# Routed attention and sorted experts on one core: a second GpSimd drain, another order of the first loads, and four smaller moves

## The chip, the cores and the metric

One core of a Trainium2 chip. Its engines are called here by the profile's names beside their own: PE (TensorE, matmuls), PEld (its weight loads), DVE (VectorE), ACT (ScalarE), POOL (GpSimd) and SP (SyncE, which here only issues transfers). The metric is the device time of one execution in microseconds. Times inside the trace are counted from the start of its span.

## The reference

Two blocks follow each other. The first is attention with a mask by clusters: each query and each key is assigned to the nearest of 16 centroids of its head, and a query only sees keys of the same cluster. The second is a layer of experts: a gate picks one of 8 experts for each of the 3072 tokens, and the token goes through that expert's two matrices.

```python
# q, k, v: (4 batches, 8 heads, 768, 64); centroids: (8, 16, 64); w1: (8, 512, 1024); w2: (8, 1024, 512)
q_assign = argmax(einsum("bhsd,hcd->bhsc", q_n, c_n), -1)   # q_n, k_n, c_n: rows divided by their norm
k_assign = argmax(einsum("bhsd,hcd->bhsc", k_n, c_n), -1)
mask = q_assign[:, :, :, None] == k_assign[:, :, None, :]
scores = where(mask, q @ k.T / 8, -1e9)
attn_out = softmax(scores) @ v
x = attn_out.transpose(0, 2, 1, 3).reshape(3072, 512)
expert_idx = argmax(x @ w_gate, 1); gate_w = softmax(x @ w_gate)[expert_idx]
y[t] = gate_w[t] * (relu(x[t] @ w1[expert_idx[t]]) @ w2[expert_idx[t]])
```

All of it is float32.

## The kernel before

**Attention.** The 16 pairs of heads (4 batches times 4 pairs) are worked off one after another. For pair n TensorE makes the scores of 12 blocks in fp32, adds the mask by a bf16 matmul of one-hot clusters (`mq`, `mk`, two buffers each, L370), ScalarE takes the exp (`A`, L383), VectorE adds the blocks up (`acc`, L389), and TensorE multiplies `A` with v (L395). Beside it, steps of the pairs to come are put between the blocks: the loads of pair n+2, the transposes of q and k (L262 for pair 0 on TensorE, L272 for the others on VectorE), the similarity to the centroids (`similar`, L304) and the one-hot clusters (`assign0` to `assign2`, `place`). In `place`, ScalarE copies the one-hot clusters of the queries into `mq` (L350, four copies a pair) and VectorE writes those of the keys into `mk` (L352).

A step is put in its place by `at_pair(n, u, f, ...)`: f is issued in pair n after block u (0 to 11 the score blocks, 12 and 13 in the attends). `sum_up` of the pair before (L415: the sums for the softmax and the gate's logits, in one PSUM bank), `weights_of` (VectorE reads that bank), `rows` and `store` (L452: the rows of x to HBM) go in this way, and so do the steps by which a batch's tokens are given to experts: `gate`, `gate_exp`, `gate_sum`, `choose` (whose last result is `last`, L521), `count` (two matmuls with 8 columns, L526 and L527, into a PSUM bank of its own out of the two of the pool `ps_m`), `number` (VectorE reads the counts, L532 and L533, and gets each token's place `pos_i`, L539; GpSimd then scatters the tokens into the list `tokens_of`, L541). `rank_first` and `first_turns` prepare the first turns from the first three batches.

**The start.** `load(0)` and `load(1)` are issued first: q and k of pair 0 in halves on SP's and ScalarE's queues (L183), v on SP's (L193), and then the eight transfers of pair 1 (L187) and its v. The centroids are normed and transposed (`cn`, `cT`), and stored in HBM as `cn_d` (L289). `routing_constants` lets GpSimd write constants (L138 to L160), among them `none`, with which SP fills `tokens_of` by eight transfers (L141).

**The experts.** The sorted tokens are worked off in ten turns: two of 288 columns from the first batches, and eight (256, 288, 288, 384, 416, 416, 448 and 128 columns), ordered by the experts' counts. A turn's layer 1 (L902) and layer 2 (L1003, L1022) are made by Strassen's scheme with seven products in place of eight, so VectorE makes sums of the weights (`w1_sums`, L723 with `a`; `w2_sums`, L723 with `v`), of the rows (`x_sums`) and of the hidden values (`h_sums`), and adds up the products (L860). The weights of a turn are fetched by `first_weights` (w1, 2 MB, L97) and `second_weights` (w2, 2 MB, L105), each in one of two buffers by the turn's parity. The tokens of a turn come by `places` (reads the list, `sf`, L646), `indices` (`gi`, `si`, L662), `gather` (GpSimd, `xg`, L672), `weigh` (L689, L695) and `take` (L705); `write` (L977) puts out the rows by GpSimd's indirect transfers. Here too a step has a place: `at(h1, i, ...)` in layer 1 of the turn, `at(h2, i, ...)` in layer 2. Buffers and semaphores follow from the order in which the steps are written; every engine executes its instructions in that order.

The last turn has 128 columns. It runs without Strassen; its output is one PSUM bank, which ScalarE copies to SBUF (L1029), GpSimd writes out, and after which every engine drains and the program ends (L1435).

Of the kernel before, what the change touches and what calls it, by code (L numbers as in the profile page):

```python
# [8 lines left out]
F32 = mybir.dt.float32  # L9
# [24 lines left out]
def kernel(  # L34
# [128 lines left out]
    with tc.manual_schedule(), ExitStack() as actx:  # L163
# [12 lines left out]
        def load(n):  # L176
            b, hp = divmod(n, HP)
            for d, src, name in ((QIN, q, "q_in"), (KIN, k, "k_in")):
                t = d[n] = ld.tile([P, NI, Q4], F32, name=name)
                if n == 0:  # L180
                    t = d[n] = t.rearrange("p i d -> p (i d)").rearrange("p (j a d) -> p j a d", a=2, d=D)
                    for a in range(2):
                        (nc.sync, nc.scalar)[a].dma_start(out=t[:, :, a, :], in_=src[0, a].rearrange("(p j) d -> p j d", j=NQ))  # L183
                    continue
                for r in range(4):
                    s = src[b, 2 * hp + r // 2, :, Q4 * (r % 2) : Q4 * (r % 2 + 1)]
                    nc.sync.dma_start(  # L187
                        out=t[Q4 * r : Q4 * (r + 1)].rearrange("t (j a) d -> t j a d", a=4),
                        in_=s.rearrange("(a t j) d -> t j a d", a=4, j=NQ),
                    )  # L190
            VIN[n] = ldv.tile([P, 2, NQ, D], F32, name="v_in")
            for a in range(2):
                nc.sync.dma_start(  # L193
                    out=VIN[n][:, a], in_=v[b, 2 * hp + a].rearrange("(p j) d -> p j d", j=NQ)
                )

        cin = consts.tile([P, D], F32)
        nc.scalar.dma_start(out=cin, in_=centroids.rearrange("h c d -> (h c) d"))
        for n in range(2):
            load(n)  # L200

# [9 lines left out]
        MK = [msk.tile([P, S], BF16, name=f"mk{i}") for i in range(2)]  # L211
        for i in range(2):
            for t in (MQ[i], MK[i]):
                (nc.gpsimd if i else nc.vector).memset(t, 0.0)

# [4 lines left out]
        for a in range(2):  # L220
# [3 lines left out]
            )  # L224
        make_identity(nc, ident)
        first_c = iota("first_c", [P, C], [[-1, C]], C, 0)
        ones_s = consts.tile([P, 2, Q4], F32)
# [57 lines left out]
        for a in range(2):  # L285
            nc.vector.tensor_copy(cT[D * a : D * (a + 1), :, a, :], cv[D * a : D * (a + 1), :, a, :])
        first_turn(1)
        for a in range(2):
            nc.scalar.dma_start(  # L289
                out=cn_d.rearrange("(h a) d c -> a d h c", a=2)[a], in_=cT[D * a : D * (a + 1), :, a, :]  # L290
            )
        first_cb = consts.tile([P, C], BF16)
        nc.vector.tensor_copy(first_cb, first_c)
        ksc2 = consts.tile([P, 2], F32)
        kscn2 = consts.tile([P, 2], F32)
        for r in range(4):
            nc.vector.tensor_copy(ksc2[Q4 * r : Q4 * (r + 1)], ksc)
            nc.vector.tensor_copy(kscn2[Q4 * r : Q4 * (r + 1)], kscn)

# [42 lines left out]
        def place(n, w):  # L342
            t, m = OH[n], (MQ, MK)[w][n % 2]
            for h in range(2):
                for a in range(2):
# [3 lines left out]
                    if w == 0:  # L349
                        nc.scalar.copy(dst, src)  # L350
                    else:
# [51 lines left out]


        def sum_up(n):

            ps = SL[n] = ps_m.tile([P, 512], F32, name="mps")
            for w in range(3):
                for qd in range(4):
# [112 lines left out]

        def count(b):
            last = LAST.pop(b)
            cps = CPS[b] = ps_m.tile([P, 512], F32, name="mps")
            nc.tensor.matmul(cps[:, 0:E], lhsT=lt_strict, rhs=last, start=True, stop=True)  # L526
# [234 lines left out]
        for n in range(NPAIR):  # L761
            if n:
                at_pair(n, 2, sum_up, n - 1)
                at_pair(n, 2, weights_of, n - 1)
                at_pair(n, 4, rows, n - 1)
# [3 lines left out]
        for b in range(B - 1):  # L769
# [3 lines left out]
            at_pair(n, 8 if last else 11, gate_exp, b)  # L773
            at_pair(n + (not last), 10 if last else 3, gate_sum, b)
            at_pair(n + (not last), 8 if last else 9, choose, b)
            at_pair(n + 2 - last, 0 if last else 4, count, b)
            at_pair(n + 2 - last, 1 if last else 6, number, b)
        n = HP * (B - 1)
        slots = range(len(EARLY))
        at_pair(n + 1, 3, rank_first)  # L780

# [46 lines left out]
    with tc.manual_schedule(), ExitStack() as ectx:  # L828
# [156 lines left out]
        def layer2(s, hooks):  # L985
# [28 lines left out]
            def tile_of(j):  # L1014
# [4 lines left out]
                for k in range(FB // n):  # L1019
# [6 lines left out]
                    if n == 1 and k % 2 and not pairs:  # L1026
                        hook()
                if n == 1:
                    nc.scalar.copy(z[0:m], ps[0:m])  # L1029
# [68 lines left out]
        for s in range(NS):  # L1098
# [5 lines left out]
            if s == 0:  # L1104
# [11 lines left out]
                at(h2, 0, rank_rest)  # L1116
                at(h2, 3, places, 2)
                at(h2, 7, indices, 2)
                at(h2, 7, gather, 2)
# [3 lines left out]
            if s < last:  # L1123
# [6 lines left out]
                if s == 1:  # L1130
                    at(h1, 6, weigh, 2)
                    at(h1, 7, take, 2)

                    at(h1, 7, first_weights, 2)
                    at(h1, 8, second_weights, 2)
# [7 lines left out]
                elif s == 1:  # L1143
                    when = ((h2, 2), (h2, 3), (h2, 4), (h2, 5), (h2, 6), (h2, 6))
                else:
# [17 lines left out]
            if pairs_of(s):  # L1163
                at(h1, 4, w2_sums, s, (1,), nc.vector)
                at(h1, 6, w2_sums, s, (3,), nc.vector)
            (layer1 if GR[s]["T"] >= 2 * P else few_columns)(s, h1)
            h_sums(s)
# [272 lines left out]
```

## Time and profile before

| | us |
|---|---|
| median of 3 runs | 679.32 |
| the runs | 682.28, 679.32, 677.63 |
| the profiled execution | 680.02 |
| its span | 678.2 |
| PE busy | 648.1 (96%) |
| DVE busy | 512.5 (76%) |
| ACT busy | 301.0 (44%) |
| POOL busy | 124.4 (18%) |
| mean granted clock of PE | 0.989 |

The first pair's scores begin at 11.9 us, a pair takes 19.7 us and some of those in which a batch is counted up to 22.2, the first turn's first matmul is at 339.3, and the last matmul ends at 666.5. A line of the profile names the source line, the engine, the operation with its output and inputs, how many times it ran, its busy time, and the idle time of its engine ahead of it with what ended that. The profiled execution is 1.8 us longer than its span; differences within the span are read from the trace and then set against the runs.

### The profile page before, as it was taken

Reading aid. Unit: us, or ns where it says so; the run is one execution under the profiler, and the core shown is the slowest. Engines: PE = TensorE matmul, PEld = TensorE weight load, DVE = VectorE, ACT = ScalarE, POOL = GpSimd, SP = SyncE. Lnnn points to the kernel's source line nnn. Section 1 sums busy time; section 2 is a strip of 40 time slices with the busy share of each in tenths; the row PEclk is TensorE's granted clock in tenths of the full one; section 3 lists DMA queues with packets and bytes.
Section 4 is the critical chain, followed back from the end, with each engine's and each line's share of the span. In section 5 each row is a group of like instructions: output and inputs, shape, how many; then the busy total and the mean of one; then the engine's idle time right before and its main releaser. Section 6 shows DMA issues by size and latency. Waiting matters only on the chain.

```text
span 678.2 us, 11364 instructions
## 1 busy us (share of the span) xinstructions
PE 648.1 (96%) x4210; PEld 424.3 (63%) x4210; DVE 512.5 (76%) x909; ACT 301.0 (44%) x524; POOL 124.4 (18%) x145
## 2 busy tenths in 40 slices
PE   4999999999999999999999989999999999999993
PEld 2445444455444454444484879978797977869771
DVE  5889999999999999999887788886868375562300
ACT  2756556667556566556432323333231332413210
POOL 4000000012000300222113522324241422040010
PEclk9899999999999999999999989999999999999997
DMA  9723455433455434356473498667494837523010
GB/s 185 144 51 73 88 94 94 67 70 69 80 94 94 73 73 78 63 152 197 113 264 96 147 388 281 227 261 251 196 288 175 271 127 218 201 73 135 7 49 17
DMA packets 191807, 95.37 MB, mean 141 GB/s; under 512 B 155967, under 2 KB 173887, under 8 KB 190464
## 3 DMA queue, kind: packets, MB, share of 16 engines
q1 hardware_dynamic: 184016, 81.12, 43.8%
q0 software_dynamic: 4928, 12.97, 5.8%
q10 hardware_dynamic: 2800, 0.48, 0.4%
q8 instruction: 35, 0.57, 0.4%
q14 instruction: 28, 0.23, 0.1%
HBM read 74.10 MB, written 20.70 MB: 140 GB/s over the span
## 4 chain that ended last, share of the span: by engine, by line
PE 52%; issue 27%; DVE 8%; DMA 5%; POOL 5%; SPq 2%; ACT 1%; POOLq 0%; DVEq 0%; ACTq 0%
PE sps L370 19%; PE mps L395 15%; PE bank L902 4%; PE bank L1003 3%; PE sbank L902 3%; POOL out_dram L977 3%; PE sbank L1003 2%; PE mps L415 2%; PE bank L1022 2%; PE mps L304 2%; DVE acc L389 2%; POOL xg L672 1%; DMA w<-in_moe_w_dram 1%; DVE a L723 1%; DVE xw L689 1%
## 5 line engine op out<-in xcount | busy, mean ns | idle before, releaser
L383 ACT ACTIVATE A<-sps 128x768 f32<-128x768 f32 x192 | 153.1, 811 | 47.3 <-PE sps L370 46.2
L370 PE MATMUL sps<-qT,kT 64*128 64x384 f32 x768 | 160.2, 496 | 1.9 <-ACT A L383 1.9
L389 DVE TENSOR_TENSOR acc<-acc,A 128x768 f32<-128x768 f32 x128 | 121.4, 948 | 9.7 <-ACT A L383 3.3
L395 PE MATMUL mps<-A,v_in 128*64 128x384 f32 x768 | 127.4, 488 | 0.0
L370 PEld LDWEIGHTS sps<-qT,kT 64*128 64x128 f32 x768 | 66.8, 188 | 57.8 <-issue 51.0
L395 PEld LDWEIGHTS mps<-A,v_in 128*64 128x64 f32 x768 | 53.8, 137 | 70.5 <-issue 62.2
L977 POOL DMA_INDIRECT out_dram<-z,si x30 | 47.8, 1594 | 199.9 <-DVE z L860 170.7
L541 POOL DMA_INDIRECT tokens_of<-tg,pos_i x24 | 27.1, 1128 | 291.8 <-DVE pos_i L539 145.8
L370 PE MATMUL sps<-mq,mk 64*128 64x384 bf16 x384 | 63.4, 324 | 2.7 <-ACT mq L350 2.7
L1022 PE MATMUL bank<-w,h 128*128 128x512 f32 (+2 forms) x224 | 64.4, 596 | 0.0
L672 POOL DMA_INDIRECT xg<-x_rows,gi x30 | 41.4, 1382 | 50.7 <-DVE gi L662 19.3
L350 ACT COPY mq<-ohT 32x384 bf16<-32x384 bf16 x64 | 32.6, 510 | 38.7 <-DVE ohT L340 29.5
L902 PE MATMUL sbank<-xc,a 128*128 128x144 f32 (+4 forms) x288 | 48.0, 310 | 1.4 <-ACT h L920 0.7
L902 PE MATMUL bank<-xT,w 128*128 128x144 f32 (+4 forms) x288 | 47.8, 309 | 0.0
L902 PEld LDWEIGHTS bank<-xT,w 128*128 128x128 f32 x288 | 43.9, 191 | 2.6 <-issue 2.2
L1022 PEld LDWEIGHTS bank<-w,h 128*128 128x128 f32 (+2 forms) x224 | 24.6, 151 | 32.5 <-issue 32.3
L902 PEld LDWEIGHTS sbank<-xc,a 128*128 128x128 f32 x288 | 43.3, 190 | 2.1 <-issue 1.2
L860 DVE TENSOR_TENSOR h<-sbank,p 128x288 f32<-128x288 f32 (+4 forms) x18 | 9.2, 513 | 46.8 <-PE sbank L902 45.7
L370 PEld LDWEIGHTS <-mk 64*128 64x128 bf16 x384 | 19.5, 94 | 28.2 <-DVE mk L352 3.3
L920 ACT ACTIVATE h<-h 128x288 f32<-128x288 f32 (+4 forms) x36 | 17.6, 488 | 41.4 <-DVE h L860 32.6
L689 DVE TENSOR_TENSOR xw<-xg,sf 128x256 f32<-128x256 f32 (+2 forms) x60 | 32.8, 607 | 2.2 <-DMA xg<-x_rows,gi 1.7
L389 DVE TENSOR_TENSOR acc<-A 128x768 f32<-128x768 f32 x32 | 30.3, 947 | 5.1 <-ACT A L383 5.0
(205 smaller groups left out, 884.5 us busy)
## 6 DMA issues: line engine op xcount, KB each, us to landing
w<-in_moe_w_dram SPq DMA_DIRECT2D x20, 2048.0 KB
v_in<-in_v_dram SPq DMA_DIRECT2D x32, 192.0 KB
x_rows<-x SPq DMA_DIRECT2D x64, 96.0 KB
turn_rows<-xw SPq DMA_DIRECT2D x23, 256.0 KB
q_in<-in_q_dram SPq DMA_DIRECT2D x60, 96.0 KB
k_in<-in_k_dram SPq DMA_DIRECT2D x60, 96.0 KB
xs<-turn_rows SPq DMA_DIRECT2D x16, 144.0 KB
xs<-turn_rows SPq DMA_DIRECT2D x8, 208.0 KB
```

Of the source, the lines that this page charges most:

```text
L350: nc.scalar.copy(dst, src)
L370: nc.tensor.matmul(SP[n, h, j][:, a, 0:HS], lhsT=kt[rows, j * P : (j + 1) * P], rhs=qt[rows, h * HS : (h + 1) * HS], start=first, stop=not ...
L383: nc.scalar.activation(A[n, h, j], ps[:, :, 0:HS], AF.Exp, scale=D**-0.5)
L389: nc.vector.tensor_tensor(ACC[n, h], first, A[n, h, j], op=ALU.add)
L395: nc.tensor.matmul(O[n, h][D * a : D * (a + 1), 0:HS], lhsT=VIN[n][:, a, j, :], rhs=A[n, h, j][:, a, :], start=(j == 0), stop=(j == NQ - 1),)
L541: ins = nc.gpsimd.indirect_dma_start(out=t_d[:, :], out_offset=bass.IndirectOffsetOnAxis(ap=pos_i[:, i : i + 1], axis=0), in_=tg[:, b, i, ...
L672: nc.gpsimd.indirect_dma_start(out=xg[0:m], out_offset=None, in_=x_d[0:rows_in, :], in_offset=bass.IndirectOffsetOnAxis(ap=g["gi"][0:m, j ...
L689: nc.vector.tensor_tensor(xw[0:m, :, :, d2 * a : d2 * (a + 1)], xg[0:m].rearrange("p (r a d b) -> p a r b d", r=HP, a=2, b=DB)[:, a], g["s ...
L902: nc.tensor.matmul(ps[:, f * T2 : (f + 1) * T2], lhsT=w[:, k, (2 * j + f) * P : (2 * j + f + 1) * P], rhs=x[:, k, :], start=first and f + ...
L977: ins = nc.gpsimd.indirect_dma_start(out=out[:, :], out_offset=bass.IndirectOffsetOnAxis(ap=GR[s]["si"][0:rows, j : j + 1], axis=0), in_=z ...
L1003: nc.tensor.matmul(ps[:, 0:H], lhsT=x[:, k, :], rhs=y[:, k, :], start=first and k == 0, stop=k == 3, skip_group_check=not first,)
L1022: nc.tensor.matmul(ps[i * m : (i + 1) * m, :], lhsT=h[:, f, j * P : j * P + m], rhs=w[:, f, :], start=(k == 0), stop=(k == FB // n - 1),)
```

## The change

Six edits stand in the diff.

1. In turn `last - 1` (turn 8, the last but one) GpSimd executes `drain` at step 4 of layer 1.
2. The first loads: v of pair 0 and all of pair 1 are issued after the centroids' transposed norms are there; these go to HBM on SP's queue, not on ScalarE's. `first_cb`, `ksc2` and `kscn2` (nine small copies) are made by GpSimd in place of VectorE, the memsets of `MQ[1]` and `MK[1]` come after `ident`, and two of pair 0's four `mq` copies go to GpSimd.
3. `count` writes into the second half of the bank that `sum_up` holds at that time, in place of a bank of its own; the steps `gate_sum`, `choose`, `count` and `number` of the attention pairs get other places, `weights_of` is issued after `count`, and `rank_first` comes a step later.
4. `first_weights(2)` goes from layer 1 of turn 1 (step 7) to layer 2 of turn 0 (step 3).
5. Of turn 2's `w1_sums`, the four go from steps 2 to 5 of turn 1's layer 2 to steps 9 and 10 of its layer 1 and 2 and 3 of its layer 2.
6. In the last turn the copy of the output is made in two halves of 256 columns, one by ScalarE and one by VectorE.

```diff
--- before.py
+++ after.py
@@ -188,6 +188,11 @@
                         out=t[Q4 * r : Q4 * (r + 1)].rearrange("t (j a) d -> t j a d", a=4),
                         in_=s.rearrange("(a t j) d -> t j a d", a=4, j=NQ),
                     )
+            if n:
+                load_v(n)
+
+        def load_v(n):
+            b, hp = divmod(n, HP)
             VIN[n] = ldv.tile([P, 2, NQ, D], F32, name="v_in")
             for a in range(2):
                 nc.sync.dma_start(
@@ -196,8 +201,7 @@
 
         cin = consts.tile([P, D], F32)
         nc.scalar.dma_start(out=cin, in_=centroids.rearrange("h c d -> (h c) d"))
-        for n in range(2):
-            load(n)
+        load(0)
 
         csq = consts.tile([P, D], F32)
         cs2 = consts.tile([P, 1], F32)
@@ -209,9 +213,8 @@
         nc.scalar.activation(warm, cnrm, AF.Exp, scale=0.0)
         MQ = [msk.tile([P, S], BF16, name=f"mq{i}") for i in range(2)]
         MK = [msk.tile([P, S], BF16, name=f"mk{i}") for i in range(2)]
-        for i in range(2):
-            for t in (MQ[i], MK[i]):
-                (nc.gpsimd if i else nc.vector).memset(t, 0.0)
+        for t in (MQ[0], MK[0]):
+            nc.vector.memset(t, 0.0)
 
         cT = consts.tile([P, HP, 2, C], F32)
         nc.vector.memset(cT, 0.0)
@@ -223,6 +226,8 @@
                 in_=moe_w_gate.rearrange("(h a d) e -> a d h e", a=2, d=D)[a],
             )
         make_identity(nc, ident)
+        for t in (MQ[1], MK[1]):
+            nc.gpsimd.memset(t, 0.0)
         first_c = iota("first_c", [P, C], [[-1, C]], C, 0)
         ones_s = consts.tile([P, 2, Q4], F32)
         nc.gpsimd.memset(ones_s, 0.0)
@@ -284,18 +289,21 @@
         cv = cps[:, 0:P].rearrange("p (h a c) -> p h a c", a=2, c=C)
         for a in range(2):
             nc.vector.tensor_copy(cT[D * a : D * (a + 1), :, a, :], cv[D * a : D * (a + 1), :, a, :])
+        for a in range(2):
+            nc.sync.dma_start(
+                out=cn_d.rearrange("(h a) d c -> a d h c", a=2)[a], in_=cT[D * a : D * (a + 1), :, a, :]
+            )
+
+        load_v(0)
+        load(1)
         first_turn(1)
-        for a in range(2):
-            nc.scalar.dma_start(
-                out=cn_d.rearrange("(h a) d c -> a d h c", a=2)[a], in_=cT[D * a : D * (a + 1), :, a, :]
-            )
         first_cb = consts.tile([P, C], BF16)
-        nc.vector.tensor_copy(first_cb, first_c)
+        nc.gpsimd.tensor_copy(first_cb, first_c)
         ksc2 = consts.tile([P, 2], F32)
         kscn2 = consts.tile([P, 2], F32)
         for r in range(4):
-            nc.vector.tensor_copy(ksc2[Q4 * r : Q4 * (r + 1)], ksc)
-            nc.vector.tensor_copy(kscn2[Q4 * r : Q4 * (r + 1)], kscn)
+            nc.gpsimd.tensor_copy(ksc2[Q4 * r : Q4 * (r + 1)], ksc)
+            nc.gpsimd.tensor_copy(kscn2[Q4 * r : Q4 * (r + 1)], kscn)
 
         def similar(n):
             ps = ps_m.tile([P, 512], F32, name="mps")
@@ -347,7 +355,8 @@
                     dst = m[D * a : D * a + Q4, HS * h : HS * (h + 1)]
                     src = t[Q4 * g : Q4 * (g + 1), :]
                     if w == 0:
-                        nc.scalar.copy(dst, src)
+
+                        (nc.gpsimd.tensor_copy if n == 0 and h else nc.scalar.copy)(dst, src)
                     else:
                         nc.vector.tensor_scalar(
                             dst, src, scalar1=ksc2[Q4 * g : Q4 * (g + 1), a : a + 1],
@@ -402,9 +411,12 @@
                 nc.scalar.copy(OT[n][:, h * HS : (h + 1) * HS], O.pop((n, h))[:, 0:HS])
 
 
+        BANK = []
+
         def sum_up(n):
 
             ps = SL[n] = ps_m.tile([P, 512], F32, name="mps")
+            BANK[:] = [ps] if n < NPAIR - 1 else []
             for w in range(3):
                 for qd in range(4):
                     if w < 2:
@@ -521,8 +533,9 @@
             nc.vector.tensor_copy(last, pr[:, :, TC - 1])
 
         def count(b):
+
             last = LAST.pop(b)
-            cps = CPS[b] = ps_m.tile([P, 512], F32, name="mps")
+            cps = CPS[b] = BANK.pop()[:, 2 * P : 4 * P] if BANK else ps_m.tile([P, 512], F32, name="mps")
             nc.tensor.matmul(cps[:, 0:E], lhsT=lt_strict, rhs=last, start=True, stop=True)
             nc.tensor.matmul(cps[:, E : 2 * E], lhsT=ones_sq, rhs=last, start=True, stop=True)
 
@@ -761,7 +774,6 @@
         for n in range(NPAIR):
             if n:
                 at_pair(n, 2, sum_up, n - 1)
-                at_pair(n, 2, weights_of, n - 1)
                 at_pair(n, 4, rows, n - 1)
                 at_pair(n, 4, store, n - 1)
             for u, step in ((2 if n else 4, 1), (5, 2), (7, 3), (8, 4), (11, 5)):
@@ -771,13 +783,15 @@
             last = b == B - 2
             at_pair(n, 5 if last else 10, gate, b)
             at_pair(n, 8 if last else 11, gate_exp, b)
-            at_pair(n + (not last), 10 if last else 3, gate_sum, b)
-            at_pair(n + (not last), 8 if last else 9, choose, b)
-            at_pair(n + 2 - last, 0 if last else 4, count, b)
-            at_pair(n + 2 - last, 1 if last else 6, number, b)
+            at_pair(n + (not last), 9 if last else 3, gate_sum, b)
+            at_pair(n + (not last), 10 if last else 9, choose, b)
+            at_pair(n + 2 - last, 2, count, b)
+            at_pair(n + 2 - last, 3 if last else 6, number, b)
+        for n in range(1, NPAIR):
+            at_pair(n, 2, weights_of, n - 1)
         n = HP * (B - 1)
         slots = range(len(EARLY))
-        at_pair(n + 1, 3, rank_first)
+        at_pair(n + 1, 4, rank_first)
 
         def first_turns():
             for s in slots:
@@ -1025,7 +1039,11 @@
                         )
                     if n == 1 and k % 2 and not pairs:
                         hook()
-                if n == 1:
+                if n == 1 and s == last:
+
+                    nc.scalar.copy(z[0:m, 0:H], ps[0:m, 0:H])
+                    nc.vector.tensor_copy(z[0:m, H:], ps[0:m, H:])
+                elif n == 1:
                     nc.scalar.copy(z[0:m], ps[0:m])
                 else:
                     for i in range(1, n):
@@ -1115,6 +1133,7 @@
                 at(h1, 12, rank_all)
                 at(h2, 0, rank_rest)
                 at(h2, 3, places, 2)
+                at(h2, 3, first_weights, 2)
                 at(h2, 7, indices, 2)
                 at(h2, 7, gather, 2)
             if s == 3:
@@ -1130,8 +1149,6 @@
                 if s == 1:
                     at(h1, 6, weigh, 2)
                     at(h1, 7, take, 2)
-
-                    at(h1, 7, first_weights, 2)
                     at(h1, 8, second_weights, 2)
                 else:
                     second_weights(s + 1)
@@ -1141,7 +1158,7 @@
                 if s == 0:
                     when = ((h2, 1), (h2, 2), (h2, 4), (h2, 5), (h2, 7), (h2, 7))
                 elif s == 1:
-                    when = ((h2, 2), (h2, 3), (h2, 4), (h2, 5), (h2, 6), (h2, 6))
+                    when = ((h1, 9), (h1, 10), (h2, 2), (h2, 3), (h2, 6), (h2, 6))
                 else:
                     when = ((h1, 9), (h1, 10), (h2, 1), (h2, 2), (h2, 2), (h2, 5))
                 if GR[s + 1]["T"] >= 2 * P:
@@ -1163,6 +1180,9 @@
             if pairs_of(s):
                 at(h1, 4, w2_sums, s, (1,), nc.vector)
                 at(h1, 6, w2_sums, s, (3,), nc.vector)
+            if s == last - 1:
+
+                at(h1, 4, nc.gpsimd.drain)
             (layer1 if GR[s]["T"] >= 2 * P else few_columns)(s, h1)
             h_sums(s)
             layer2(s, h2)
```

More of the change, by code (lines that the diff above doesn't have):

```diff
@@ L286 @@
             nc.vector.tensor_copy(cT[D * a : D * (a + 1), :, a, :], cv[D * a : D * (a + 1), :, a, :])
-        first_turn(1)
         for a in range(2):
-            nc.scalar.dma_start(
+            nc.sync.dma_start(
                 out=cn_d.rearrange("(h a) d c -> a d h c", a=2)[a], in_=cT[D * a : D * (a + 1), :, a, :]
             )
+        load_v(0)
+        load(1)
+        first_turn(1)
         first_cb = consts.tile([P, C], BF16)
-        nc.vector.tensor_copy(first_cb, first_c)
+        nc.gpsimd.tensor_copy(first_cb, first_c)
         ksc2 = consts.tile([P, 2], F32)
```

## The prediction

> **What bounds the kernel now.** I read the page's parts 1 and 2 first, then the waits of TensorE in order of size, then each of those places in the timeline, and last what stands after the last matmul.
>
> ```profile
> PE 648.1 (96%) x4210; PEld 424.3 (63%) x4210; DVE 512.5 (76%) x909; ACT 301.0 (44%) x524; POOL 124.4 (18%) x145
> ```
>
> TensorE is busy for 648.1 of 678.2 us. So a change can only win in the 30 us in which it isn't, in spells of half clock, or by leaving matmuls out (this one leaves none out). TensorE's waits:
>
> ```profile
> PE sps L262 <- POOL kscn L241: 5.1, 1, 5.1
> PE sps L370 <- ACT mq L350: 2.7, 2, 2.5
> PE sbank L1003 <- DVE z L860: 2.6, 3, 2.0
> PE sps L370 <- ACT A L383: 1.9, 3, 1.2
> PE sps L262 <- DMA k_in<-in_k_dram: 1.6, 1, 1.6
> PE mps L304 <- DVE run L533: 1.5, 1, 1.5
> ```
>
> The columns are total, times and longest. Five of these lie in the first 19 us, one (L304) is before pair 14 at 280.8, one (L1003's 2.0) at 398.85 in turn 1. The stretches around that last one (PE, PEld, DVE, ACT and POOL busy, clock, DMA share, GB/s):
>
> ```profile
> 390.00:400.90 10.90, 8.88 (x44) 7.50 (x41) 7.59 (x12) 3.12 (x7) 0.93 (x1) 1.00 0.99 370
> 400.90:404.30 3.40, 3.40 (x8) 2.77 (x9) 3.38 (x4) 0.00 (x0) 1.73 (x1) 0.50 1.08 450
> 404.30:410.00 5.70, 5.70 (x52) 5.67 (x52) 5.55 (x10) 2.28 (x7) 1.45 (x1) 1.00 0.84 333
> ```
>
> After the stall the clock is 0.50 for 3.4 us: the eight L1003 matmuls there take 3.66 us where the eight before the stall took 1.89. The stall's cause is in VectorE's timeline:
>
> ```profile
> 398.00 1.23 DVE L723 TENSOR_TENSOR a<-w 128x1024 f32<-128x1024 f32 x1 [1.77 <-DMA w<-in_moe_w_dram]
> 399.26 1.23 DVE L723 TENSOR_TENSOR a<-w,a 128x1024 f32<-128x1024 f32 x1
> 400.40 0.42 DVE L860 TENSOR_TENSOR z<-sbank,p 128x256 f32<-128x256 f32 x1
> ```
>
> Turn 2's w1 lands at 397.97, two sums of it come next in VectorE's order, and only then the add that TensorE needs. The end of the run:
>
> ```profile
> 665.51 1.02 PE L1022 MATMUL bank<-w,h 128*128 128x512 f32 x2
> 666.57 0.59 ACT L1029 COPY z<-bank 128x512 f32<-128x512 f32 x1 [6.59 <-PE bank L1022]
> 667.43 0.97 POOL L977 DMA_INDIRECT out_dram<-z,si  x1 [13.04 <-ACT z L1029]
> ...
> L1435 POOLq DRAIN  x3: 46/107/6934, 670.4 to 677.9; - x3
> L1435 SPq DRAIN  x3: 7/7/13, 671.4 to 677.6; - x3
> ...
> L1426 POOLq DRAIN  x1: 194/194/194, 0.4 to 0.4; - x1
> ```
>
> The last output has landed at 670.67, yet the run ends at 678.2, because GpSimd's closing drain alone takes 6.93 us from 670.4. At the start, with no transfer of its own behind it, the same instruction took 0.194. Of the 678.2, then, 18.2 us are TensorE's gaps, some 3.4 its half clock, and 11.7 the tail.
>
> **What the Trainium skill says.** "VectorE: DVE Perf Modes", section "The DRAIN you can't avoid", gives the drains at a program's two ends as about 12 ns on all engines. SyncE's 7 to 13 ns agree; GpSimd's 6934 doesn't, and no page has a price for it. "TensorE: Matmul & The Clock Gate", Part 1, says that the clock halves after an idle window and returns after about 3.4 us of work; the spell above lasted 3.4 us, but an idle of 2.0 us was enough. "DMA: Bandwidth & Descriptors", section "Issuing engines are not separate DMA queues", says that all transfers share the same 16 engines; k_in's second half, behind v_in of the same pair, landed at 8.29 and its first at 6.25. "PSUM — Partial Sum Buffer", section "PSUM bank collisions raise a hardware error", says that two engines may not touch one bank's quadrant at once, reads included; the trace agrees: ScalarE's zt copy starts at 368.58 and 391.41, just after VectorE's add out of the same bank ended (368.55, 391.37).
>
> **The change part by part.**
>
> *GpSimd's second drain.* Put at layer 1's step 4 of turn 8, it lies in GpSimd's idle of 610.5 to 636.7 (26.2 us): even at 6.9 us nothing queues behind it. The trace has only one drain after transfers, so what its length follows is unknown. If it follows GpSimd's indirect DMAs since the last drain (84: 30 gathers, 30 outputs, 24 scatters), 79 move to the middle and 5 outputs stay: 0.194 + 6.74 x 5/84 = 0.60 us, ending at 671.0. Then SyncE's drain at 671.4 is late next; what follows the 6.93 now lasts 0.8, so the end is 672.2: 6.0 us won. If its length is fixed, 0. A loss is excluded by the 26 us of cover. I take 6.0, because 0.19 against 6.93 for one instruction speaks for work left over; range 0 to 6.4.
>
> *First loads.* v_in of pair 0 (384 KB from about 4.9 us) goes behind cn_d, and pair 1's loads behind that. Without it in front, k_in is in by about 6.4 (from bytes left and the 250 KB/us of that stretch), before cn's transpose ends at 6.82: L262's wait of 1.6 goes. The first wait, 5.1, stays: q_in's second half lands at 4.96, while ident was ready at 3.62, so the memsets moved behind it win nothing. VectorE's nine small copies (10.45 to 11.48) lay in its own wait for `sim`: 0. Of the four mq copies on ScalarE (0.52 each, 16.04 to 18.14) two go to GpSimd in parallel; the first exp started at 18.16 though its score was ready near 17.5: 0.65 of L383's 1.2. Less idle should save some 0.15 of the half clock at 18.6 to 22.0. Sum 2.4, range 1.0 to 2.6. The cost: GpSimd's routing constants (4.95 to 9.65 before) stand behind those copies, from about 14.2 to 20; SP waits for cT (7.6) with cn_d, then issues v_in, eight loads of pair 1 at 0.70 until 15.7, then the eight fills of tokens_of and pair 2. Pair 1's k lands near 17.8 (14.45 before) and TensorE wants it turned near 19.8: about 0.9 us to spare after VectorE's turn. Pair 2 is needed at 36.07 and landed near 25; 4 us later still fits.
>
> *Counts in the sums' bank.* The L304 wait of 1.50 goes, as `similar` no longer needs the bank that `run` L533 reads; for batches 0 and 1 only an order of short matmuls (0.39 and 0.37 at 350) changes. But VectorE has no gap over 0.1 us from 240.7 to 329.7 and only one until 347: it sets the pace there, and TensorE merely runs ahead to wait later. I take 0.2 (0 to 1.5). `number` moves from step 1 to 3, so the last scatters are up to 3 us later and the tokens' first read about 0.9 (295.5 to 296.4); its user, the indices at 302.76, has about 1.5 to spare.
>
> *Turn 2's weights in turn 0.* w1(2) is issued near 365.9 instead of 389.04. Its buffer, w1(0)'s, is free at about 356, and the DMA engines are almost empty from 369 to 378, so it lands near 373. sf(3), issued at 366.9, goes behind 2 MB to about 373.5; VectorE wants it at 377.8. The wait of 1.77 and the sums ahead of the L860 add leave turn 1's second half: TensorE gains 2.0, and 3.66 - 1.89 = 1.8 of half clock. Against it, the first two sums (2 x 1.23) now stand in layer 1 at steps 9 and 10, where later turns show TensorE gaps of 0.55 and 0.7: -0.5. Net 3.3, range 1.5 to 3.8.
>
> *Last copy.* 586 ns of ScalarE become 128x256 on ScalarE (0.37, as L1076) and 128x256 on VectorE (0.42, as L860). Both read one bank, so I take them one after the other: 0.37 + 0.42 = 0.79, a loss of 0.2; in parallel a gain of 0.17.
>
> **Sum.** 6.0 + 2.4 + 0.2 + 3.3 - 0.2 = 11.7 us. The profiled execution took 680.0 (span 678.2), so 668.3; it lies 0.7 above the median of 679.32, so 667.6, said as 668.
>
> **The rivals.**
>
> *A: the drain's length is fixed.* For it: two other drains at the end took 46 and 107 ns, so the long one may be a fixed closing job. Against: 0.194 at the start. Gain 5.7, so 673.6, said as 674.
>
> *B: VectorE takes the rest back.* It sets the pace in pairs 11 to 14 and in turn 0, so the start's gain is partly lost there (VectorE's own work starts only some 0.8 earlier), and turn 1 keeps half its stall. Gain 6.0 + 0.8 + 1.8 - 0.2 = 8.4: 671. Against: in pairs 0 to 5 TensorE has no waits and VectorE has idle.
>
> *C: slower, by SP's order at the start.* SP executes in order, and pair 2's loads stand behind the fills of tokens_of, which wait for a memset of GpSimd that now waits for the mq copies. I put that at 15; should it come at 38, pair 2 would land 12 us later, at 50 (3.5 for the fills, 5.6 for its issues, 3 to land), 13.9 after VectorE wants it; with 1.7 of half clock that is 15.6 lost, so 680.0 - 11.7 + 15.6 = 683.9, against the median 683. It decides from 24 on and passes the time before at 34. For it: GpSimd gets the waits of ten more copies ahead. Against: the same operations took 4.7 us in all before.
>
> **How the numbers follow.** My forecast has 0.57, with its own range 665 to 671; A 0.20, B 0.17, C 0.06. A change under about 1% (672.5 to 686.1) can't be told from none by a measurement of this kernel. Faster by over 1%: 0.56 of my case, 0.15 of B and 0.02 of A: 0.73. Slower: 0.04 of C, whose fills may come later than priced. Within 1%: the rest, 0.01 of mine, 0.02 of B, 0.18 of A and 0.02 of C: 0.23. The range: down to 664.5, about where every gain is at its upper bound (6.4 + 2.6 + 1.5 + 3.8 + 0.2 = 14.5: 664.8 against the median); up to 675, which takes in A. Left out are C and the edges, about 0.15.
>
> **What would show it.** Right: a long GpSimd drain near 612, a closing one under 1 us, and 5 to 6 us between the last matmul and the end; no L262 wait on k_in; w1(2) issued near 366, and no half clock near 400. Wrong: a closing drain of 6 us or more; a TensorE wait on kT near 19 or 36; SP waiting for w1's buffer near 366, with sf(3) behind it.

## The result, and the profile after

The changed kernel took 672.03 us (median of 6 runs, 670.74 to 673.18) against 678.80 of the kernel before (6 runs, 677.47 to 682.28). The quotient of these medians is 0.9900. The ratio estimated from the runs, with its 95% interval, is 0.9887 (0.9868 to 0.9905); the ratios below are of this kind too, and not quotients of the medians. So the kernel is about 1% faster, where 668 had been forecast in a range of 664.5 to 675. Measured again later, it took 671.58 against 679.94. In the profiled execution (672.25, span 670.7) the page's first part reads:

```profile
PE 649.9 (97%) x4210; PEld 425.7 (63%) x4210; DVE 512.3 (76%) x901; ACT 300.0 (45%) x522; POOL 127.3 (19%) x156
```

The matmuls are the same 4210. TensorE's waits, in order of size (total, times, longest; the lines of the source have moved, L370 is now L379, L902 is L916, L860 is L874):

```profile
PE sps L267 <- POOL first_cb L301: 5.2, 1, 5.2
PE sbank L916 <- DVE h L874: 3.4, 3, 2.4
PE sps L379 <- DVE mk L361: 2.6, 2, 2.4
PE mps L427 <- DVE acc L398: 0.9, 2, 0.7
PE sbank L1017 <- DVE z L874: 0.6, 2, 0.4
PE sps L379 <- ACT A L392: 0.6, 1, 0.6
```

Gone are the wait for k_in, the one for `run`, and the 2.0 us of turn 1's second layer. The first wait stays, as forecast. New is a wait of 2.4 us for `h`. VectorE's timeline shows where it is and why:

```profile
382.52 1.21 DVE L736 TENSOR_TENSOR v<-w,v 128x1024 f32<-128x1024 f32 x1
383.65 1.22 DVE L736 TENSOR_TENSOR a<-w 128x1024 f32<-128x1024 f32 x1
384.97 1.23 DVE L736 TENSOR_TENSOR a<-w,a 128x1024 f32<-128x1024 f32 x1
386.11 0.45 DVE L874 TENSOR_TENSOR h<-sbank,p 128x288 f32<-128x288 f32 x1
```

TensorE is free at 384.20 and needs the add of 386.11. The two `a` sums ahead of it are those that the change put at steps 9 and 10. After the stall the clock is at half for 3.4 us (the columns are PE, PEld, DVE, ACT and POOL busy, clock, DMA share, GB/s):

```profile
380.00:386.60 6.60, 4.21 (x35) 3.99 (x33) 5.47 (x7) 1.19 (x4) 4.70 (x4) 1.00 0.70 239
386.60:390.10 3.50, 3.48 (x12) 3.21 (x13) 1.20 (x3) 1.58 (x4) 0.00 (x0) 0.51 0.77 207
```

So the stall near 399 with its half clock went, and one of the same kind came 14 us earlier. The end:

```profile
662.91 1.02 PE L1036 MATMUL bank<-w,h 128*128 128x512 f32 x2
663.97 0.37 ACT L1044 COPY z<-bank 128x256 f32<-128x256 f32 x1 [6.59 <-PE bank L1036]
664.37 0.42 DVE L1045 COPY z<-bank 128x256 f32<-128x256 f32 x1 [22.52 <-ACT z L1044]
665.08 0.97 POOL L991 DMA_INDIRECT out_dram<-z,si  x1 [13.29 <-DVE z L1045]
```

And GpSimd's drains by their lines, at the program's end and in turn 8 (count, shortest, median and longest in ns, first and last start):

```profile
L1455 POOLq DRAIN  x3: 46/107/2229, 666.5 to 669.8; - x3
...
L1120 POOLq DRAIN  x1: 10250/10250/10250, 606.7 to 606.7; - x1
```

The closing drain fell from 6.93 to 2.23 us; the added one takes 10.25 us in the middle (606.7 to 616.9), and GpSimd's next output only comes at 634. The instruction that GpSimd executes just ahead of its closing drain became shorter too, before and after:

```profile
L1174 POOLq INC_SWDGE_SEM  x1: 1872/1872/1872, 668.5 to 668.5; - x1
L1194 POOLq INC_SWDGE_SEM  x1: 289/289/289, 666.2 to 666.2; - x1
```

How far each kernel had come at a few places (start of the k-th matmul in the trace, counted from 0, then the last output's issue and the end of the span, in us):

| | 400th | 2000th | 2600th (turn 0) | 3600th | last output | end |
|---|---|---|---|---|---|---|
| before | 67.50 | 279.05 | 363.88 | 538.23 | 667.43 | 678.22 |
| changed | 65.83 | 276.87 | 362.89 | 535.64 | 665.08 | 670.65 |
| mended (last experiment) | 65.59 | 276.71 | 363.08 | 532.97 | 662.16 | 666.85 |

The changed kernel gains 1.7 us by pair 2, 2.2 by pair 13, has 1.0 left in turn 0, gains 1.6 in turns 1 to 5 and 5.2 behind the last output.

### The profile page after: what moved, and what is told of

Its sections match the earlier page's. It is cut to its first block, busy times and chain, and to the rows that moved or that the text cites. A ratio compares the mean times of both kernels' runs of the same rounds, so it can differ in the third digit from the quotient of the medians.

```text
span 670.7 us, 11366 instructions
## 1 busy us (share of the span) xinstructions
PE 649.9 (97%) x4210; PEld 425.7 (63%) x4210; DVE 512.3 (76%) x901; ACT 300.0 (45%) x522; POOL 127.3 (19%) x156
## 3 DMA queue, kind: packets, MB, share of 16 engines
q0 software_dynamic: 4928, 12.97, 5.8%
## 4 chain that ended last, share of the span: by engine, by line
PE 77%; issue 9%; DVE 7%; POOL 2%; DMA 2%; ACT 1%; POOLq 0%; SPq 0%; DVEq 0%; ACTq 0%
PE sps L379 20%; PE mps L404 15%; PE bank L916 9%; PE sbank L916 7%; PE bank L1017 7%; PE bank L1036 7%; PE sbank L1017 5%; PE mps L427 2%; PE mps L312 2%; DMA xg<-x_rows,gi 1%; PE bank L885 1%; DVE acc L398 1%; DVE v L736 1%; DVE xT L727 1%; POOL tokens_of L554 1%
## 5 line engine op out<-in xcount | busy, mean ns | idle before, releaser
L379 PE MATMUL sps<-qT,kT 64*128 64x384 f32 x768 | 159.3, 494 | 0.6 <-ACT A L392 0.6
L379 PEld LDWEIGHTS sps<-qT,kT 64*128 64x128 f32 x768 | 67.1, 188 | 55.0 <-issue 51.4
L379 PE MATMUL sps<-mq,mk 64*128 64x384 bf16 x384 | 63.5, 325 | 2.6 <-DVE mk L361 2.6
L916 PE MATMUL sbank<-xc,a 128*128 128x144 f32 (+4 forms) x288 | 48.0, 310 | 0.2
L916 PE MATMUL bank<-xT,w 128*128 128x144 f32 (+4 forms) x288 | 47.8, 309 | 0.0
L874 DVE TENSOR_TENSOR h<-sbank,p 128x288 f32<-128x288 f32 (+4 forms) x18 | 9.2, 512 | 48.3 <-PE sbank L916 48.3
L916 PEld LDWEIGHTS bank<-xT,w 128*128 128x128 f32 x288 | 43.8, 191 | 2.6 <-issue 2.2
L916 PEld LDWEIGHTS sbank<-xc,a 128*128 128x128 f32 x288 | 43.3, 191 | 0.9 <-ACT sbank L940 0.6
L379 PEld LDWEIGHTS <-mk 64*128 64x128 bf16 x384 | 19.5, 95 | 28.0 <-DVE mk L361 3.4
```

Of the source, the lines that this page charges most:

```text
L379: nc.tensor.matmul(SP[n, h, j][:, a, 0:HS], lhsT=kt[rows, j * P : (j + 1) * P], rhs=qt[rows, h * HS : (h + 1) * HS], start=first, stop=not ...
L916: nc.tensor.matmul(ps[:, f * T2 : (f + 1) * T2], lhsT=w[:, k, (2 * j + f) * P : (2 * j + f + 1) * P], rhs=x[:, k, :], start=first and f + ...
```

## The experiments

Single runs of one kernel lie up to 2 us or more from its median, so the small edits are judged by the traces. A trace is one execution too, and is set beside the others where they bear on the same stretch.

**The drain alone, and everything but the drain.** Two kernels: the one before with this edit only, and the changed one without it.

```diff
+            if s == last - 1:
+                at(h1, 4, nc.gpsimd.drain)
```

> The kernel before with the second drain of GpSimd alone, nothing else of the change. Theory (the closing drain is as long as the transfers that GpSimd issued since its last drain, plus the landing of the last one): the drain in turn 8 takes 7 to 10 us in GpSimd's idle, the closing one about 2.2 us, TensorE's last matmul stays at 666.5, and the time falls by 4.5 to 5.5 us to about 673.7. Rival (the closing drain became short by something else in the change, such as the split last copy or the earlier landing): it stays at 6.9 us and the time at about 678.8.

> The changed kernel without its second drain. Theory: the closing drain is about 6.9 us again and the time rises by 4.5 to 5.5 us to about 677. Rival (something else shortened it): about 672, with a closing drain near 2.2 us.

The drain alone: 673.76 against 680.4, ratio 0.9913 (0.9886 to 0.9939). All but the drain: 677.54, ratio 0.9962 (0.9951 to 0.9974). The closing drains of the first, and then those of the second:

```profile
L1438 POOLq DRAIN  x3: 46/107/1860, 668.2 to 671.1; - x3
```

```profile
L1452 POOLq DRAIN  x3: 46/107/6934, 666.2 to 673.7; - x3
```

The second has to the nanosecond the 6934 of the kernel before. From the last output's issue to the end it is 10.78 us before and 10.79 without the drain, 4.66 with the drain alone and 5.57 in the changed kernel; over all twelve traces with an added drain it lies between 4.66 and 5.98. So the drain is worth 4.8 to 6.1 us in the traces. By the medians it is 6.6 where it is added to the kernel before, and 5.5 where it is taken from the changed one. The theory held, and most of what the change brings is this one instruction.

**What a drain's length follows.**

```diff
-            if s == last - 1:
-                at(h1, 4, nc.gpsimd.drain)
+            if s in (2, 4, 6, 7, 8):
+                at(h1, 4, nc.gpsimd.drain)
+            if s == 8:
+                at(h1, 4, nc.gpsimd.drain)
```

> The changed kernel with GpSimd drains at step 4 of layer 1 in turns 2, 4, 6, 7 and 8, and in turn 8 two of them one after the other. Theory (a drain takes some 0.08 to 0.13 us for each transfer that GpSimd issued since the last one, and waits for the landing of the last): the first, after some 40 transfers, takes 4 to 7 us, the next ones, after 5 to 14 each, 1 to 4 us, the second of the two in turn 8 under 0.3 us, and the closing one about 2 us. Rival (a drain's length is fixed once any transfer was issued, and the landing comes on top): 7 us or more for each but the second of the pair.

A single run took 671.63 (span 670.0). The six drains in the turns, and then the closing three (shortest, median, longest in ns):

```profile
L1120 POOLq DRAIN  x6: 53/7286/11027, 403.8 to 613.2; - x6
...
L1456 POOLq DRAIN  x3: 46/107/455, 668.4 to 669.6; - x3
```

The second of the pair took 0.053 us: with nothing behind it a drain is short. The others are long mainly because they also wait for transfers still on their way. Counted from the end of the last packet of GpSimd's queue to the end of the drain, with n the indirect transfers since the last drain, the traces fall near two lines. Where the drain began before that last packet: n = 79: 3.61 to 3.65 us in eleven traces; 41: 2.08; 15: 1.30; 14: 0.95; 5: 0.67 to 0.86; 4: 0.56. That is about 0.5 us and 0.04 for each transfer. Where it began after the packet, its own duration is 6.93 at n = 84 and 0.455 at n = 5: 0.08 to 0.09 for each, and nearly nothing besides, though only these two counts show it. The fixed length (rival A) falls. Packets rise with the transfers (4928 for the 84), and no run varied the two apart; counted by packets the first line bends, 0.6 ns for each between n = 41 and 79 and 0.8 below. The first drain took 5.48 us, as I had expected. The next ones I had put at 1 to 4 us, and they took 7.1 to 11.0, as the landings came on top. The short closing drain of this run brought no earlier end: it began 3.92 us after the last output's issue, instead of 1.44 in the changed kernel, and the end came 5.57 us after that issue in both.

**The sums of turn 2's w1, and their fetch.**

```diff
-                    when = ((h1, 9), (h1, 10), (h2, 2), (h2, 3), (h2, 6), (h2, 6))
+                    when = ((h2, 2), (h2, 3), (h2, 4), (h2, 5), (h2, 6), (h2, 6))
```

> The changed kernel with turn 2's four sums of w1 back at steps 2 to 5 of turn 1's layer 2, while its w1 is still fetched in turn 0. Theory (the changed kernel's new stall of 2.42 us at 384.2 and the half clock after it come from the two sums that stand ahead of the add of h in VectorE's order): the stall and its half clock go, the old stall near 398 doesn't come back as w1 is there, TensorE ends some 4 us earlier, and the time is about 668. Rival (VectorE is late at 384 because its rows come late, behind the 2 MB of w1): a stall of over 1 us stays there and the time is 670.5 to 672.

For the next, `first_weights(2)` also went back to step 7 of turn 1's layer 1.

> The changed kernel with both the fetch of turn 2's w1 and its sums where they were before. Theory (the two edits swap one stall of TensorE for another of the same size): the stall near 384 goes, one of about 2 us near 397 with half clock after it returns, and the time is 671.5 to 673. Rival (the early fetch is worth its 3.3 us and the stall at 384 has another cause): about 675.

With the sums late and the fetch early: 670.71, ratio 0.9870 (0.9837 to 0.9903); with both undone: 673.31, ratio 0.9902 (0.9872 to 0.9932). In the first, the time is short of the 668 that I had expected, and lies in the rival's range. But the stall near 384 is gone, which the rival had staying there. The old one near 398 is 0.16, and 0.96 and 0.51 come up at 405 and 413, since VectorE now has no idle time from 391 to 407. In the second, waits of 0.90, 1.13, 0.74 and 1.05 stand at 398, 406, 414 and 436, with no half clock. From the 2600th to the 3600th matmul it is 173.3 us with both undone (174.4 in the kernel before, 172.9 in it with the drain alone), 172.7 in the changed kernel and 170.9 with late sums. So the early fetch is worth 2.4 us in this stretch and 2.6 by the medians, and the two sums at steps 9 and 10 gave 1 to 2 us of it back. The stall of 2 us with half clock that I had expected near 397 of the second run didn't return, so the two edits weren't a full swap, but together worth 1.3 by the medians.

**The last copy.** ScalarE alone again:

```diff
-                if n == 1 and s == last:
-
-                    nc.scalar.copy(z[0:m, 0:H], ps[0:m, 0:H])
-                    nc.vector.tensor_copy(z[0:m, H:], ps[0:m, H:])
-                elif n == 1:
+                if n == 1:
```

> The changed kernel with its last copy by ScalarE alone again. Theory (the two halves run one after the other, as both read one bank): from the end of the last matmul to the start of the last output's transfer it is 0.2 to 0.3 us shorter, about 0.9 instead of 1.1 us, and the time 671.8. Rival (the halves overlap or the handover is free): this stretch is 0.2 us longer and the time 672.2. The runs can't tell these times apart, the trace can.

670.65, ratio 0.9884 (0.9854 to 0.9914), not told from the changed kernel. The trace is plain:

```profile
662.54 0.58 ACT L1043 COPY z<-bank 128x512 f32<-128x512 f32 x1 [6.59 <-PE bank L1036]
663.40 0.97 POOL L991 DMA_INDIRECT out_dram<-z,si  x1 [13.04 <-ACT z L1043]
```

From ScalarE's start to the output's issue it is 0.86 us with one copy and 1.11 with two (663.97 to 665.08). GpSimd's idle time before this last output is 13.29 us in each trace with two copies and 13.04 in each with one. The split costs 0.25, as VectorE's copy starts (664.37) only after ScalarE's has ended (664.34).

**The counts.** Bank, places of the gate's steps and order of `weights_of` as before (the core of the edit):

```diff
-            cps = CPS[b] = BANK.pop()[:, 2 * P : 4 * P] if BANK else ps_m.tile([P, 512], F32, name="mps")
+            cps = CPS[b] = ps_m.tile([P, 512], F32, name="mps")
```

> The changed kernel with counts in a bank of their own and the old places of the gate's steps. Theory (VectorE sets the pace from pair 11 to turn 0, so what TensorE gains there is waited away): the stall of 1.5 us near 279 returns, the one of 0.71 near 298 goes, by the first turn the two kernels are within 0.4 us of each other, and the time is 672 to 672.5. Rival (the edit is worth its whole stall): TensorE is 1.5 us later at the first turn and the time is 673.5 or more.

672.86, ratio 0.9895 (0.9859 to 0.9932). The wait is back, and the 0.71 for `acc` near 298 is gone:

```profile
PE mps L312 <- DVE run L546: 1.5, 1, 1.5
```

From the 400th to the 2600th matmul it takes 297.8 us, the changed kernel 297.1. But the eleven traces with the edit spread from 296.2 to 297.9 there (mean 297.0), and the three without it have 296.4, 297.1 and 297.8 (mean 297.1). So the edit takes away a wait of 1.5 us and brings one of 0.7, and what is left of it can't be told from nothing; the medians, 0.8 to 1.3 apart, don't show more.

**The start.** All of edit 2 undone, and then only the two `mq` copies given back to ScalarE.

```diff
-            if n:
-                load_v(n)
...
-        load(0)
+        for n in range(2):
+            load(n)
...
-                        (nc.gpsimd.tensor_copy if n == 0 and h else nc.scalar.copy)(dst, src)
+                        nc.scalar.copy(dst, src)
```

> The changed kernel with the first loads, the small copies, the memsets and the four mq copies as before. Theory (the start is worth some 1.7 us at pair 0, of which VectorE's bound stretch takes a part back): TensorE is 0.5 to 1.7 us later in the pairs, 0.5 to 1.2 later in the first turn, and the time is 672.5 to 673.2. Rival (all of the predicted 2.4 us are there): 674.4.

> The changed kernel with all four mq copies of pair 0 by ScalarE. Theory (the first exp waits for ScalarE's copies): the wait of TensorE for the first exps is 1.2 us instead of 0.6, pair 0's later scores are some 0.6 us later counted from its ohT, and the time is not told from the changed kernel's. Rival (another wait, on VectorE's mk copies, hides it): the waits and the distance stay as in the changed kernel.

All undone: 674.11, ratio 0.9917 (0.9894 to 0.9941), 2.1 above the changed kernel by the medians, with runs from 670.2 to 677.5. The 400th matmul starts at 66.77 there, at 67.50 and 67.52 in the two traces of the old start beside it, and between 65.05 and 66.06 in the ten traces with the whole new start: 1.8 us between the means (67.26 and 65.47). Half clock in the first 25 us differs from trace to trace; where it lasts 3.4 us the old start has 67.50 and the new one 65.49 (mean of nine), and where there is none 66.77 and 65.27, which leaves 1.5 to 2.0. The waits with the old start:

```profile
PE sps L262 <- DMA k_in<-in_k_dram: 2.3, 1, 2.3
PE sps L371 <- ACT mq L351: 1.6, 2, 1.4
PE sps L371 <- ACT A L384: 1.2, 1, 1.2
```

The k_in wait is 2.3 here, 1.60 in the kernel before and 0.55 in the one with the drain alone, as k_in's second half lands at 8.90, 8.29 and 7.32. In the eleven traces with v behind it, it lands between 6.5 and 7.0, and no wait for it is left. The kernel with the drain alone, for all its short wait, is no earlier at the 400th matmul; its clock was at half for 6.8 us from 16.3, not for 3.4. In the changed kernel the next wait, for the masks, is 2.4 us (VectorE's four `mk` copies from 14.81 to 16.84), where it was 1.4 here and 2.5 in the kernel before. With the copies back on ScalarE (a single run, 670.22), the wait for the first exps is 1.25 us instead of 0.57, as expected.

**Mended.** One copy at the end, and one of the four sums at the end of layer 1, where VectorE idles, three in layer 2:

```diff
-                    when = ((h1, 9), (h1, 10), (h2, 2), (h2, 3), (h2, 6), (h2, 6))
+                    when = ((h1, 12), (h2, 2), (h2, 3), (h2, 4), (h2, 6), (h2, 6))
```

> The changed kernel with one copy at the end, and with turn 2's sums of w1 one at step 12 of turn 1's layer 1 and three at steps 2 to 4 of its layer 2. Theory (the stall at 384 comes from two sums ahead of the add of h, those near 405 and 413 of the kernel with all four sums late from too much work for VectorE between 394 and 406): none of the three is there with over 0.6 us, TensorE's end lies 4 to 5 us ahead of the changed kernel's profiled one (which had half clock as well), and the time is 669 to 670. Rival (the work only moves): a stall of over 1 us elsewhere in turns 1 and 2, and about 670.7 as with all four late.

> The changed kernel once more, beside its mended form, on the same chip. Theory: its stall in turn 1 is again 2.4 to 2.6 us, with half clock after it in some executions and not in others; about 672. Rival (the stall of 2.42 was chance): under 1 us.

> The changed kernel with one copy at the end and turn 2's sums at step 12 of turn 1's layer 1 and steps 2 to 4 of its layer 2, again. Theory: 2 to 3 us under the changed kernel, 669 to 670.5, and no stall in turn 1. Rival (the difference of the traces was chance at the start): within 1 us of it.

The first time 670.68, ratio 0.9888 (0.9854 to 0.9923). That missed the 669 to 670 that I had expected and fits the rival's time, though no stall of over 1 us came up elsewhere, as the rival had it. 0.69 was left near 410, and TensorE ended 3.4 us earlier than in the changed kernel, not 4 to 5. The second time, beside each other, the changed kernel took 671.58, ratio 0.9886 (0.9859 to 0.9912), and the mended one 669.63, ratio 0.9857 (0.9836 to 0.9878): 2.0 us less. Its ten runs together have a median of 669.7, the twelve of the changed kernel 671.8. The same stretches as above, in its second trace:

```profile
380.00:386.60 6.60, 6.59 (x50) 6.25 (x50) 4.74 (x8) 2.67 (x7) 3.90 (x4) 1.00 0.74 246
386.60:390.10 3.50, 3.50 (x24) 1.63 (x23) 2.91 (x6) 0.93 (x2) 0.00 (x0) 1.00 0.76 195
```

TensorE is busy throughout at full clock; of the stalls in turns 1 and 2, 0.52 is left near 412. From the 2600th to the 3600th matmul it takes 169.9 us. In the changed kernel's repeat the stall was 2.52, with no half clock after it.

## Why the prediction was right, and where it was not

The median fell by 6.8 us, and by 8.4 in the repeat, where the sum had said 11.7. Its sign and its place in the range came out right, and the mechanism that carries most of it, the drain, was the right one. The range was wide, as it took in rival A as well, and in size the result lies nearer to rival B (8.4, 671) than to the forecast. Of the signs that were named, four came: a long GpSimd drain near 612, no wait for k_in, w1 issued near 366 (at 365.61), and no half clock near 400. Two didn't: the closing drain isn't under 1 us, and from the last matmul to the end it is 6.7 us and not 5 to 6 (5.6 with the drain alone).

*The drain: right, in part by luck.* Predicted 6.0; 5.2 in the profiled pair, 5.5 to 6.6 by the medians with and without it. That a drain settles the transfers issued since the last one is what the runs show: where it began after the last landing, it took 0.455 after 5 transfers, near the 0.60 of the sum. In the changed kernel it is 2.23, because it starts while the last output is still on its way and ends 0.7 us after its last packet. It starts so early because the instruction ahead of it is 1.58 us shorter (0.289 for 1.872), which the prediction hadn't seen. The two misses cancel: the drain ends 3.7 us after the last output's issue, where 3.6 had been put (671.0 less 667.43). The added drain takes 10.25 us, more than the 6.9 that I had allowed, within 26 us of cover.

*Turn 2's weights: the step that failed.* "Against it, the first two sums now stand in layer 1 at steps 9 and 10, where later turns show TensorE gaps of 0.55 and 0.7: -0.5." The fetch itself came as worked out: w1 landed at 373.17 and the list behind it at 373.50. But the term of 0.5 measured 2.4 to 2.6 us in seven of the eight traces with these places and 1.4 in the eighth (the one with the `mq` copies on ScalarE), and 1.7 more where half clock followed. I had taken the price from later turns. But turn 1 also has two pairs of `xw` products for the next turn's tokens and a `v` sum just ahead (379 to 383.7, with 0.63 and 0.99 us of waiting for the gathered rows), so VectorE reaches the sums as TensorE already nears the add. What stands just ahead of the add in turn 1 isn't in the prediction. Moved out, the sums leave nearly what the step had promised: 3.0 us between the traces with late sums and those with fetch and sums in their old places (170.5 and 173.5, means of three each), against 3.3 predicted. With the sums at steps 9 and 10 it is 1.5 (172.0, mean of eight).

*The start: size.* Predicted 2.4, measured 1.8. The k_in wait was priced at its 1.6 in one profile, where two other executions of the same start had 0.55 and 2.3. The 0.65 for the `mq` copies was right. Rival C didn't come about: SP issued the fills of `tokens_of` at 16.96, near the 15 that I had put.

*The counts: right.* 0.2 predicted, 0.1 between the means of the traces, with a spread of over 1 us. VectorE does take back what TensorE gains there, as I had written into this step and into rival B: of the 2.2 us gained by the 2000th matmul 1.0 is left in turn 0 (of 2.6 some 1.8 by the means of all traces with the whole change up to there), though the wait of 1.5 went in between. The gap of 0.71 near 298 is a part of it.

*The last copy: right.* A loss of 0.2 predicted, 0.25 measured, with one copy after the other. The two places that the prediction named as showing the same, at 368.58 and 391.41, don't show it: there the engines read different rows of the bank (VectorE rows 0 to 31, ScalarE 64 to 95), so they only show that the copy waited.

So of the 11.7, the weights of turn 2 missed some 2, the start 0.6, and VectorE took about 1; that leaves 8, beside the 6.8 and 8.4 measured. Rival B's number came near, but not all of its reasons: VectorE took some of the start's gain, as B had said, while the stall in turn 1 is a new one of the sums' order.

## What to carry to other kernels

Look at what stands behind the last matmul: where a core has issued many indirect transfers by GpSimd (84 here), a drain in a long idle stretch of GpSimd settles most of them early. When work is moved ahead in an engine's order, price it by what stands just ahead of the next instruction that the bound engine waits for, in that very stage, and not by the idle time of the stage or by the same places in another. A wait read from one profile is worth what the next wait lets through, and a wait on a transfer at the start varies between executions.

## What the runs showed of the hardware

A GpSimd drain's length follows the number of its indirect transfers since the last one: 0.08 to 0.09 us for each where all had landed (6.93 at 84, 0.455 at 5), 0.05 to 0.2 with none (0.053 just behind another drain, 0.194 at the program's start), and landings come on top. INC_SWDGE_SEM, just ahead of the closing drain, took 1.87 us after 84 transfers without a drain and 0.29 to 0.30 with one in between.

An idle of 2.4 to 2.6 us of TensorE at the same place was followed by half clock in two executions (2.42, 2.55) and not in five others (2.52 to 2.59), all in kernels with the same code there. The half clock cost 1.7 us: sixteen matmuls (eight L916, eight L1017) took 2.27 + 2.60 us instead of 1.25 + 1.89. The idle's length doesn't decide; its place in time does. In each trace with more than one spell of half clock the starts lie whole multiples of 3.413 us apart: at 18.57, 400.86 and 670.51 in the kernel before (112 and 79 of them), at 18.04, 386.68 and 666.58 in the changed kernel (108 and 82). Cut the time into windows on this grid, and the stalls differ in how much of them falls into one window. In the changed kernel all of the 2.42 us did, and the next window had half clock. In its repeat, 1.92 of the 2.52 fell into one window and 0.60 into the next, and the clock stayed full:

```profile
383.27:386.68 3.41, 0.99 (x9) 0.78 (x7) 3.19 (x4) 0.08 (x1) 2.04 (x2) 1.00 0.69 235
...
381.30:384.71 3.41, 1.49 (x13) 1.27 (x11) 3.31 (x4) 0.00 (x0) 2.71 (x2) 1.00 0.74 231
384.71:388.12 3.41, 2.81 (x16) 2.42 (x16) 1.81 (x5) 1.47 (x4) 0.00 (x0) 1.00 0.73 189
```

Over all fourteen traces, from 25 us on, each of the 18 windows with 2.01 us or more of idle was followed by half clock, four of them in the turns (2.01 before, 2.02 with the drain alone, 2.42 and 2.55), and none of the 2606 with 1.92 or less. In the first 25 us windows with 1.6 and 1.8 us were followed by it too, so the border isn't shown for there. The grid lies elsewhere in each execution, so one and the same stall costs 1.7 us more or not by chance, and this can be a part of the spread between runs of one kernel.
